# The first tokens' u half of a gated MLP by seven block products in place of eight, in a planned kernel

## The chip, the cores and the metric

The kernel runs on one core of a Trainium2 chip. The metric is device microseconds of one execution. Times are in microseconds (us) unless a text says otherwise.

## What is computed

Three layers in float32, for B = 2 batches, S = 768 tokens and a model width of 512 (8 heads of 64):

```python
for t in range(S):                       # retention, per head
    state = gamma * state + outer(k[t], v[t])
    y[t] = scale * (q[t] @ state)
# spectral mixing over tokens, then channels
theta = x @ w_theta
yr = einsum('ts,bsd->btd', w_tok_r, x * cos(theta))
yi = einsum('ts,bsd->btd', w_tok_i, x * sin(theta))
u = x + yr + yi
x = u + maximum(u @ w_ch, 0.0)
# gated MLP
h = gelu_tanh(x @ w_in)                  # 512 -> 1024
u, v = h[..., :512], h[..., 512:]
v_n = (v - mean(v)) / sqrt(var(v) + 1e-06) * g_ln
v_s = einsum('ts,bsd->btd', w_sg, v_n) + b_sg[None, :, None]
return x + (u * v_s) @ w_out
```

The change concerns `x @ w_in[:, :512]`, the u half.

## The kernel before, in words

**Precision.** Every operand of a large product is split into a high and a low half of a shorter float32 format: ScalarE rounds to the high half (`split_hi`, L331) and VectorE subtracts to get the low one (`split_lo`, L337). `terms3` then multiplies high by high, low by high and high by low: three matmuls for each 128-deep block, all recorded at L311. Weights come as 64-bit words and are unpacked on ScalarE (L403) and VectorE (L412, L423) before they are split.

**Tiling.** Activations lie with channels on the 128 partitions and tokens along the free axis. There are three token groups: the first 512 tokens of batch 0 (`xa[0]`), of batch 1 (`xa[1]`), and the last 256 of both (`xb`). A tile of a layer (`layer`) is 128 output channels by 512 tokens: 4 input blocks times 3 terms, 12 matmuls of 512 columns, into one of 8 PSUM banks.

**Stages.** For 12 chunks of 128 tokens: `retention` (scores, VectorE's masks at L503, the state's outer product, "attend" in a part by the state and a part by the masked scores) and `theta` (the angle product with two W_THETA blocks, sine and cosine on ScalarE, a transpose of x at L716). `mix_main` and `mix_rest` mix tokens. `channels` is the layer with w_ch, whose relu and add on VectorE (L845) make x2. `up_v` makes v tiles with tokens on partitions, `norm` and `norm_tile` normalize them, `up_u` makes the u tiles (a `layer`, then `gelu`: ScalarE square, VectorE L865, ScalarE tanh, VectorE L881). `gate_tile` mixes v over tokens and multiplies by u; `finish` and `finish_four` are the output layer.

**Seven products.** The output layer of the first tokens already has a block form in the kernel before. Input and output channels are cut in two halves each and the two batches take the place of the columns, so that a 2x2 by 2x2 block product needs seven products of blocks in place of eight. `sum_weights` makes four sums of weight blocks, `sum_tokens` four differences of token blocks, for each of two 128-channel pieces; each is split in halves as any operand is. `seven` runs the products (6 matmuls each) for j = 0, 1 in four banks, where the second product into a bank adds to the first; `both` saves the first pair's sum (a copy on ScalarE at L1139, an add on VectorE at L1144). `finish_four` adds up the results.

**Order.** Every step is an operation of `Plan` with an engine, a length and the buffers it uses. `ORDER` is a table of operation numbers; `Plan.schedule` walks it, gives each operation a start from the lengths and the buffers that come free, and the instructions are issued in the order of these starts. The engines then run their queues and wait by semaphores. Before 34 us of the plan (`WARM`), gaps in TensorE's queue are filled with matmuls on the identity whose results nobody reads (`keep_warm`). SP issues the loads and stores, POOL a state update and a few small steps.

Of the kernel before, what the change touches and what calls it, by code (L numbers as in the profile page):

```python
# [14 lines left out]
ALU = mybir.AluOpType  # L15
# [47 lines left out]
class Plan:  # L63
# [105 lines left out]


ORDER = [
# [48 lines left out]
]  # L220


# [1 line left out]
def retention_spectral_gmlp(  # L224
# [38 lines left out]
    def halves(dtype=F32):  # L263
        b = Buf("pair", dtype)
        return Half(b, 0), Half(b, 1)
# [35 lines left out]
    def x_tile(g, d):  # L301
        return xa[g][:, d, :] if g < B else xb[:, d].rearrange("p b t -> p (b t)")
# [546 lines left out]
        dve(512, relu, ps=True, r=[t], w=x_keys(g, e), prio=prio)  # L849
        split_x(x2hl, g, e, prio)  # L850

    def gelu(t, o, prio):

        s = Buf()
        act(
            512,
            lambda: A.activation(out=ap(s), in_=ap(t), func=AF.Square),  # L857
            ps=True,
            r=[t],
            w=[s],  # L860
            prio=prio,
        )
        dve(
            512,
            lambda: V.scalar_tensor_tensor(  # L865
                out=ap(s), in0=ap(s), scalar=1.0 / GA, in1=ap(t), op0=ALU.add, op1=ALU.mult
            ),
            ps=True,
            r=[t],
            w=[s],  # L870
            prio=prio,
        )
        act(
            512,
            lambda: A.activation(out=ap(s), in_=ap(s), func=AF.Tanh, scale=GA * GC),  # L875
            w=[s],
            prio=prio,
        )
        dve(
            512,  # L880
            lambda: V.scalar_tensor_tensor(  # L881
                out=ap(o), in0=ap(s), scalar=1.0, in1=ap(t), op0=ALU.add, op1=ALU.mult
            ),
            ps=True,
            r=[t, s],
            w=[o],
            prio=prio,
        )
# [91 lines left out]
    def up_u(g, f, prio):  # L980
        t = layer(W_INU, x2hl, g, f, prio)
        if f % 2 == 0:
            gu[g, f], gu[g, f + 1] = halves()
        gelu(t, gu[g, f], prio)
# [118 lines left out]
                split(res[i, n], lambda i=i, t=t: ap(t[i]), 512, prio, [t[i]])  # L1103
        return res

    def seven(base, src, hl, ws, ts, j, prio):

        z, w, x, y = (bank() for _ in range(4))

# [50 lines left out]
    def store(g, d, o, prio):  # L1160
# [10 lines left out]

        dma(256, put, r=[o], prio=prio)

    def finish_four(j, ws, ts, prio):
        z, x, y, u, v = seven(W_OUT, None, ghl, ws, ts, j, prio)

        def add(o, a, b, r, **k):
            dve(
# [88 lines left out]
    t = TE  # L1267
    for k in range(2):
        weight(W_INU + k, t - 10 + 5 * k)
        weight(W_INV + k, t - 7 + 5 * k)  # L1270
    for g in range(3):
        for e in range(NP):
            channels(g, e, t)
            t += 2.7
    for g in (0, 2, 1):
        for q in range(4):
            up_v(g, q, t)
            t += 2.7
        norm(g, t)
        for q in range(4):  # L1280
            norm_tile(g, q, t + 1)
        for f in range(NP):
            up_u(g, f, t)
            t += 2.7
    dma(384, lambda: nc.sync.dma_start(out=brow, in_=bvec), w=["brow"], prio=t - 20)
    dma(2, lambda: nc.sync.dma_start(out=gcol, in_=gvec), w=["gcol"], prio=t - 20)

# [6 lines left out]
        weight_sg(s, t - C['SGP'] + s)  # L1294
    for k in range(2):
        weight(W_OUT + k, t + 20 + 5 * k)
    for g in (2, 0, 1):
        for f in range(NP):
            gate_tile(g, f, t)
            t += 4.1  # L1300
# [116 lines left out]
```

## Time and profile before

| | |
|---|---|
| median of 3 runs | 370.33 us (369.91 to 370.38) |
| the profiled execution | 370.23 us, of which the span from first to last instruction is 368.5 |
| busy: TensorE / VectorE / ScalarE / POOL | 363.0 / 290.1 / 178.6 / 10.8 us |
| matmul records | 2,364 |
| granted TensorE clock, mean | 1.000 |
| DMA traffic | 39.08 MB; 306 to 413 GB/s in the first 55 us, under 230 after |

How to read it: a matmul's busy time includes its way through the array, so consecutive ones overlap; the step from one start to the next tells how fast they go. A float32 matmul that is not in the split format leaves two records. Most matmuls have one source line, L311, because a helper issues them, and are told apart by shape: 128x512 and 128x256 are the layers, 64x128 with 64 rows the scores, 64x64 the outer products.

### The profile page before, as it was taken

The page shows a single profiled execution, that of the slowest core. Times are in us where ns is not written, and L with a number is a line of the kernel's source. Part 1 is how long each engine was busy: PE and PEld are TensorE (multiplying, and loading weights), DVE is VectorE, ACT ScalarE, POOL GpSimd, SP SyncE. Part 2 cuts the span into 40 slices and gives each one's busy share as a digit, 9 for nine tenths or more (in the row PEclk, how much of TensorE's full clock was granted, in tenths as well). Part 3 has the DMA queues.
Part 4 walks back from the last instruction along what each step waited for, and adds up shares of the span by engine and source line. Part 5 has one row for each costly group of instructions (what it writes and reads, how often), then busy time and mean ns, then how long its engine had stood idle before and what let it go on. Part 6 is the DMA issues. An engine that isn't in the chain of part 4 may idle for free.

```text
span 368.5 us, 5764 instructions
## 1 busy us (share of the span) xinstructions
PE 363.0 (99%) x2364; PEld 311.7 (85%) x2364; DVE 290.1 (79%) x441; ACT 178.6 (48%) x298; POOL 10.8 (3%) x18
## 2 busy tenths in 40 slices
PE   8899999999999999999999999999999999999996
PEld 7788888788998988889988888888888889988885
DVE  3999999998886885775786434897999596899984
ACT  2767987742543566634343212437493744314300
POOL 1021010030001000000000000000000000000000
PEclk9999999999999999999999999999999999999999
DMA  7999990233433121414160000000000000000134
GB/s 306 410 413 407 410 384 6 88 141 121 166 114 116 34 84 34 166 30 161 68 223 6 2 0 0 2 1 0 0 2 0 0 2 1 3 0 2 58 114 171
DMA packets 10346, 39.08 MB, mean 106 GB/s; under 512 B 1360, under 2 KB 2384, under 8 KB 7888
## 3 DMA queue, kind: packets, MB, share of 16 engines
q1 hardware_dynamic: 10176, 38.67, 27.7%
q8 instruction: 18, 0.29, 0.3%
q10 hardware_dynamic: 144, 0.05, 0.1%
q14 instruction: 8, 0.07, 0.1%
HBM read 35.57 MB, written 3.15 MB: 105 GB/s over the span
## 4 chain that ended last, share of the span: by engine, by line
PE 95%; DMA 4%; DVE 0%; SPq 0%; issue 0%
PE banks L311 93%; DMA b<-qkv 3%; PE banks L716 1%; DMA dec<-decays 1%; DVE b L1231 0%; SPq L457 0%
## 5 line engine op out<-in xcount | busy, mean ns | idle before, releaser
L311 PE MATMUL banks<-b,b 128*128 128x512 f32 (+2 forms) x1776 | 327.3, 351 | 0.0
L311 PEld LDWEIGHTS banks<-b,b 128*128 128x128 f32 (+1 forms) x1776 | 276.4, 183 | 46.0 <-issue 1.2
L331 ACT ACTIVATE b<-b 128x512 fp32r<-128x512 f32 (+1 forms) x71 | 56.0, 815 | 67.4 <-DVE b L423 23.5
L337 DVE TENSOR_TENSOR b<-b,b 128x512 fp32r<-128x512 f32 (+1 forms) x71 | 62.4, 898 | 15.4 <-ACT b L331 9.2
L423 DVE SCALAR_TENSOR_TENSOR b<-b 128x1024 int32<-128x1024 int32 x32 | 38.8, 1224 | 0.8 <-ACT b L403 0.3
L331 ACT ACTIVATE b<-xa 128x512 fp32r<-128x512 f32 (+1 forms) x26 | 17.1, 670 | 25.4 <-DVE xa L845 15.9
L403 ACT ACTIVATE b<-b 128x1024 f32<-128x1024 f32 x16 | 18.6, 1160 | 11.6 <-DMA b<-wts 8.6
L857 ACT ACTIVATE b<-banks 128x512 f32<-128x512 f32 x24 | 13.7, 589 | 15.0 <-PE banks L311 15.0
L337 DVE TENSOR_TENSOR b<-xa,b 128x512 fp32r<-128x512 f32 (+1 forms) x26 | 19.1, 743 | 1.7 <-ACT b L331 1.6
L311 PE MATMUL banks<-b 64*128 64x128 f32 (+1 forms) x352 | 19.3, 256 | 0.8 <-DMA b<-qkv 0.8
L875 ACT ACTIVATE b<-b 128x512 f32<-128x512 f32 x24 | 14.7, 625 | 10.8 <-DVE b L865 10.8
L311 PEld LDWEIGHTS banks<-b 64*128 64x128 f32 (+1 forms) x352 | 17.1, 165 | 3.0 <-DMA b<-qkv 1.1
L865 DVE SCALAR_TENSOR_TENSOR b<-b,banks 128x512 f32<-128x512 f32 x24 | 15.9, 680 | 4.1 <-ACT b L857 4.1
L881 DVE SCALAR_TENSOR_TENSOR b<-b,banks 128x512 f32<-128x512 f32 x24 | 16.4, 682 | 2.6 <-ACT b L875 2.5
L724 DVE TENSOR_TENSOR b<-banks,b 128x1024 f32<-128x1024 f32 x12 | 14.7, 1223 | 3.9 <-ACT b L707 2.2
L526 ACT ACTIVATE b<-b,dec 128x64 f32<-128x64 f32 x56 | 14.1, 335 | 7.4 <-DMA b<-qkv 7.4
L503 DVE TENSOR_TENSOR b<-banks,causal 128x512 f32<-128x512 f32 x24 | 15.8, 686 | 1.7 <-PE banks L311 1.7
L412 DVE TENSOR_SCALAR b<-b 128x1024 int32<-128x1024 int32 x16 | 11.4, 717 | 4.2 <-DMA b<-wts 4.2
L331 ACT ACTIVATE b<-xb 128x512 fp32r<-128x512 f32 (+1 forms) x13 | 8.4, 663 | 12.3 <-DVE xb L845 8.7
L1036 DVE SCALAR_TENSOR_TENSOR b<-banks,gcol,brow 128x512 f32<-128x512 f32 x12 | 8.9, 749 | 5.5 <-PE banks L311 5.5
L845 DVE SCALAR_TENSOR_TENSOR xa<-banks,xa 128x512 f32<-128x512 f32 x8 | 5.5, 690 | 8.0 <-PE banks L311 7.9
L311 PE MATMUL banks<-b,state 64*64 64x128 f32 x160 | 10.9, 275 | 0.0
(66 smaller groups left out, 193.2 us busy)
## 6 DMA issues: line engine op xcount, KB each, us to landing
b<-wts SPq DMA_DIRECT2D x16, 1024.0 KB, 4.9
b<-qkv SPq DMA_DIRECT2D x24, 512.0 KB, 11.1
out<-b SPq DMA_DIRECT2D x11, 256.0 KB, 2.1
b<-wsg SPq DMA_DIRECT2D x9, 256.0 KB, 7.0
xa<-wts SPq DMA_DIRECT2D x2, 1024.0 KB, 11.2
xb<-wts SPq DMA_DIRECT2D x1, 1024.0 KB, 8.3
brow<-bvec SPq DMA_DIRECT2D x1, 384.0 KB, 11.4
dq<-qdecays SPq DMA_DIRECT2D x1, 256.0 KB, 6.4
```

The source lines that it names most:

```text
L311: nc.tensor.matmul(out=o, lhsT=l, rhs=r, start=start, stop=stop, skip_group_check=more)
L331: act(words, lambda: A.activation(out=hi(), in_=src(), func=AF.Copy), prio=prio, r=r, **k)
L337: lambda: E.tensor_tensor(out=lo(), in0=src(), in1=hi().bitcast(F32), op=ALU.subtract),
L403: lambda: A.activation(out=words(1).bitcast(F32), in_=words(1).bitcast(F32), func=AF.Copy, scale=REBIAS),
L423: lambda scalar=scalar, op=op: V.scalar_tensor_tensor(out=words(0), in0=words(1), scalar=scalar, in1=words(0), op0=op, op1=ALU.bitwise_or,),
L503: V.tensor_tensor(out=ap(at[i])[:, h * 512 + lo : h * 512 + hi].rearrange("p (n t) -> p n t", n=n), in0=ap(sc[h])[:, lo:hi].rearrange("p ( ...
L526: A.activation(out=v, in_=v, func=AF.Copy, scale=dk[:, h : h + 1])
L724: V.tensor_tensor(out=z2, in0=ap(tp)[:, None, :].to_broadcast([P, 2, 512]), in1=z2, op=ALU.mult)
L857: lambda: A.activation(out=ap(s), in_=ap(t), func=AF.Square),
L865: lambda: V.scalar_tensor_tensor(out=ap(s), in0=ap(s), scalar=1.0 / GA, in1=ap(t), op0=ALU.add, op1=ALU.mult),
L875: lambda: A.activation(out=ap(s), in_=ap(s), func=AF.Tanh, scale=GA * GC),
L881: lambda: V.scalar_tensor_tensor(out=ap(o), in0=ap(s), scalar=1.0, in1=ap(t), op0=ALU.add, op1=ALU.mult),
```

## The change

The u half of the first 512 tokens of both batches goes through `seven` as the output layer does. The operations: `sum_weights` and `sum_tokens` are called on W_INU and x2, and `up_four` adds the products up to the four results of each j and sends them through `gelu`; three of the four results now lie in SBUF, so `gelu` gets a switch that tells the planner so. `up_u` remains for the group `xb`. The weights of u are wanted earlier than those of v, u comes before v, and the gate takes the groups in the order 0, 2, 1. `ORDER` is a new table.

```diff
 ORDER = [
-    56, 58, 57, 85, 86, 59, 0, 114, 113, 60, 141, 142, 63, 62, 64, 61, 741, 87, 66, 7, 90, 88, 169,
...
+    56, 58, 57, 86, 85, 59, 113, 114, 0, 60, 169, 141, 63, 62, 64, 61, 197, 90, 65, 66, 142, 87, 7,
...
-    def gelu(t, o, prio):
+    def gelu(t, o, prio, ps=True):
...
-            ps=True,
+            ps=ps,
...
-    def seven(base, src, hl, ws, ts, j, prio):
+    def seven(base, hl, ws, ts, j, prio):
...
+    def up_four(j, ws, ts, prio):
+        z, x, y, u, v = seven(W_INU, x2hl, ws, ts, j, prio)
+        for g, f, part in ((0, j, z), (1, j, x), (0, 2 + j, y), (1, 2 + j, v)):
+            if f % 2 == 0:
+                gu[g, f], gu[g, f + 1] = halves()
+            t = part
+            if part is not z:
+                t = v if part is v else Buf()
+                dve(
+                    512,
+                    lambda t=t, part=part: V.tensor_tensor(
+                        out=ap(t), in0=ap(part), in1=ap(u), op=ALU.add
+                    ),
+                    ps=part is not v, r=[part, u], w=[t], prio=prio,
+                )
+            gelu(t, gu[g, f], prio, ps=part is z)
+
     def finish_four(j, ws, ts, prio):
-        z, x, y, u, v = seven(W_OUT, None, ghl, ws, ts, j, prio)
+        z, x, y, u, v = seven(W_OUT, ghl, ws, ts, j, prio)
...
         weight(W_INU + k, t - 10 + 5 * k)
-        weight(W_INV + k, t - 7 + 5 * k)
+        weight(W_INV + k, t + 30 + 5 * k)
     for g in range(3):
         for e in range(NP):
             channels(g, e, t)
             t += 2.7
+    ws = sum_weights(W_INU, t - 8)
+    ts = sum_tokens(lambda g, d: (lambda: x_tile(g, d), x_keys(g, d)), t - 4)
+    for f in range(NP):
+        up_u(2, f, t)
+        t += 2.7
+    for j in range(2):
+        up_four(j, ws, ts, t)
+        t += 9.5
     for g in (0, 2, 1):
         for q in range(4):
             up_v(g, q, t)
...
-        for f in range(NP):
-            up_u(g, f, t)
-            t += 2.7
...
-    for g in (2, 0, 1):
+    for g in (0, 2, 1):
         for f in range(NP):
             gate_tile(g, f, t)
```

Three places show how the instructions move. The first is SP's queue at the start, where `qkv` halves (512 KB) and W_THETA's first block (into `xb`) are loaded. Before:

```order
L457 DMA b_102<-qkv 128x1024
L482 DMA dq<-qdecays 128x512
L392 DMA xb<-wts 128x2048
L457 DMA b_106<-qkv 128x1024
L457 DMA b_108<-qkv 128x1024
```

Now:

```order
L461 DMA b_102<-qkv 128x1024
L486 DMA dq<-qdecays 128x512
L461 DMA b_105<-qkv 128x1024
L461 DMA b_107<-qkv 128x1024
L396 DMA xb<-wts 128x2048
```

The first W_THETA block stands two qkv halves further back.

The second is TensorE's queue up to the first angle product, a row of 128x512. 128x128 on a `b` buffer are scores, 64x64 an outer product, 64x128 an attend, `ident` alone a filler, `ident,xa` a transpose. Before:

```order
L311 MATMUL banks<-ident 128x128 x2
L716 MATMUL banks<-ident,xa_86 128x128 x4
L311 MATMUL banks<-b_102 64x64 x8
L311 MATMUL banks<-b_100,state_65 64x128 x8
L311 MATMUL banks<-b_166,b_102 64x128 x8
L311 MATMUL banks<-ident 128x128
L311 MATMUL banks<-b_108 128x128 x8
L311 MATMUL banks<-b_106 64x64 x8
L311 MATMUL banks<-b_121 128x128 x8
L311 MATMUL banks<-b_108,state_64 64x128 x8
L311 MATMUL banks<-b_247,b_106 64x128 x8
L311 MATMUL banks<-b_235,b_179 128x512 x2
```

Now:

```order
L315 MATMUL banks<-b_100 64x64 x8
L315 MATMUL banks<-b_105 128x128 x8
L315 MATMUL banks<-b_102,state_65 64x128 x8
L315 MATMUL banks<-b_183,b_100 64x128 x8
L315 MATMUL banks<-b_105,state_64 64x128 x8
L315 MATMUL banks<-b_223,b_107 64x128 x8
L315 MATMUL banks<-b_107 64x64 x8
L315 MATMUL banks<-b_121 128x128 x8
L720 MATMUL banks<-ident,xa_86 128x128 x8
L315 MATMUL banks<-b_123 128x128 x8
L315 MATMUL banks<-b_139 128x128 x8
L315 MATMUL banks<-b_278,b_173 128x512 x2
```

Two blocks of scores and one of transposes (four matmuls) more stand ahead of the angle product, and the third filler is gone.

The third is VectorE's queue in the channels' stage, up to the low halves for the first product on a token difference. L849 (L845 before) is the relu, L1099 a token difference, L341 a low half (L337 before); `xa_86` is batch 0, `xa_87` batch 1. Before, where the first relus of batch 0 stand:

```order
L845 SCALAR_TENSOR_TENSOR xa_86<-banks,xa_86 128x512
L337 TENSOR_TENSOR b_1906<-xa_86,b_1906 128x512
L337 TENSOR_TENSOR b_1831<-xb,b_1831 128x512
L845 SCALAR_TENSOR_TENSOR xa_86<-banks,xa_86 128x512
L845 SCALAR_TENSOR_TENSOR xb<-banks,xb 128x512
L337 TENSOR_TENSOR b_1911<-xa_86,b_1911 128x512
```

Now:

```order
L1099 TENSOR_TENSOR b_1930<-xa_87,xa_86 128x512
L849 SCALAR_TENSOR_TENSOR xa_86<-banks,xa_86 128x512
L1099 TENSOR_TENSOR b_1945<-xa_87,b_1930 128x512
L341 TENSOR_TENSOR b_1886<-xb,b_1886 128x512
L1099 TENSOR_TENSOR b_1948<-xa_87,xa_86 128x512
L341 TENSOR_TENSOR b_1892<-b_1572,b_1892 128x512
L341 TENSOR_TENSOR b_1963<-b_1948,b_1963 128x512
L341 TENSOR_TENSOR b_1965<-b_1930,b_1965 128x512
```

Seven rows run from the second batch-0 relu to the low half `b_1965`, which the first product on a token difference reads; 24 matmuls of two channel tiles stand on TensorE between that relu's tile and the product.

## Rows read from the trace of the kernel before

**Rows 1.** The page: span, and busy time of each engine.

```profile
span 368.5 us, 5764 instructions
...
PE 363.0 (99%) x2364; PEld 311.7 (85%) x2364; DVE 290.1 (79%) x441; ACT 178.6 (48%) x298; POOL 10.8 (3%) x18
```

**Rows 2.** The chain that ended last, in order of time: start, length (us), what.

```profile
5.12 11.40 DMA b<-qkv
...
49.24 0.44 PE banks L716 x4
...
130.49 234.79 PE banks L311 x1188
```

**Rows 3.** The waits of TensorE: total us, times, longest.

```profile
PE banks L311 <- DVE halfpi L273: 1.2, 1, 1.2
PE banks L311 <- DMA b<-qkv: 0.8, 2, 0.6
```

**Rows 4.** Timeline of TensorE, 200 to 222 us.

```profile
199.64 22.60 PE L311 MATMUL banks<-b,b 128*128 128x512 f32 x99
```

**Rows 5.** Timeline of TensorE, 3.5 to 20 us: start, us, instructions; idle before and releaser.

```profile
6.66 1.78 PE L311 MATMUL banks<-b 128*64 128x64 f32 x32
...
9.39 0.71 PE L311 MATMUL banks<-ident 128*128 128x128 f32 x4
...
10.84 0.69 PE L311 MATMUL banks<-b 128*64 128x64 f32 x16
11.46 1.09 PE L311 MATMUL banks<-b,state 64*64 64x128 f32 x16
12.48 1.09 PE L311 MATMUL banks<-b,b 128*64 128x128 f32 x16
...
16.56 1.16 PE L311 MATMUL banks<-b 64*128 64x128 f32 x16 [0.64 <-DMA b<-qkv]
17.65 1.09 PE L311 MATMUL banks<-b,state 64*64 64x128 f32 x16
18.67 1.52 PE L311 MATMUL banks<-b,b 128*64 128x128 f32 x17
```

**Rows 6.** The page and the DMA view: GB/s in 40 slices; a load of qkv.

```profile
GB/s 306 410 413 407 410 384 6 88 141 121 166 114 116 34 84 34 166 30 161 68 223 6 2 0 0 2 1 0 0 2 0 0 2 1 3 0 2 58 114 171
...
b<-qkv SPq DMA_DIRECT2D x24, 512.0 KB, 11.1
```

**Rows 7.** Timeline of TensorE, 37 to 49 us: three blocks of scores in a row.

```profile
38.40 2.95 PE L311 MATMUL banks<-b 64*128 64x128 f32 x48
41.28 1.09 PE L311 MATMUL banks<-b,state 64*64 64x128 f32 x16
```

**Rows 8.** Timeline of all engines, 9 to 20 us: the steps of a W_THETA block; two masks.

```profile
11.57 1.20 ACT L403 ACTIVATE xb<-xb 128x1024 f32<-128x1024 f32 x1 [0.56 <-DMA xb<-wts]
...
12.80 2.91 DVE L423 SCALAR_TENSOR_TENSOR xb<-xb 128x1024 int32<-128x1024 int32 x2
...
15.63 1.28 DVE L503 TENSOR_TENSOR b<-banks,causal 128x512 f32<-128x512 f32 x2
15.75 1.14 ACT L331 ACTIVATE b<-xb 128x1024 fp32r<-128x1024 f32 x1 [0.88 <-DVE xb L423]
...
17.42 1.22 DVE L337 TENSOR_TENSOR b<-xb,b 128x1024 fp32r<-128x1024 f32 x1
17.54 0.63 ACT L331 ACTIVATE b<-xa 128x512 fp32r<-128x512 f32 x1 [0.66 <-DVE xa L622]
```

**Rows 9.** Busy time by stretch: PE, PEld, DVE, ACT, POOL; granted clock; DMA.

```profile
134.00:154.00 20.00, 20.00 (x89) 16.54 (x89) 13.12 (x14) 12.30 (x18) 0.00 (x0) 1.00 0.26 93
...
194.00:214.00 20.00, 20.00 (x90) 16.57 (x89) 10.55 (x17) 6.22 (x10) 0.00 (x0) 1.00 0.00 1
214.00:234.00 20.00, 20.00 (x90) 16.57 (x89) 9.02 (x15) 4.93 (x10) 0.00 (x0) 1.00 0.00 0
```

**Rows 10.** The same view at the start.

```profile
10.00:20.00 10.00, 9.05 (x136) 7.45 (x136) 9.59 (x14) 7.83 (x23) 1.56 (x2) 1.00 1.02 405
```

More of the change, by code (lines that the diff above doesn't have):

```diff
@@ L867, in gelu @@
             ),
-            ps=True,
+            ps=ps,
             r=[t],
@@ L883, in gelu @@
             ),
-            ps=True,
+            ps=ps,
             r=[t, s],
```

98 rows, old and new, of the table ORDER are left out of this document.

## The prediction

> **What bounds the kernel now.** I read the busy times first, then the chain of waits, then TensorE's own waits and its timeline, and last VectorE's load by stretch. TensorE is busy 363.0 us of a 368.5 us span, VectorE 290.1, ScalarE 178.6 [rows 1]. A busy TensorE need not be a full one, so the chain matters more: after a load that lands at 16.5 us it is TensorE alone, with a last piece of 234.79 us and 1,188 matmuls that nothing interrupts [rows 2]. TensorE's two longest entries in the table of waits are 1.2 us for VectorE's first memset and 0.8 us for qkv loads, both before 17 us [rows 3]. And it is dense: 99 matmuls of 512 columns start within 22.60 us, 0.228 us each [rows 4]. So from 20 us on, a matmul taken away is time taken away, provided that VectorE and ScalarE, which make every operand, stay ahead. Before 20 us TensorE is short of data: it runs filler matmuls on the identity, at 9.39 for one, and waits before 16.56 [rows 5].
>
> **Twelve matmuls fewer.** The first tokens' u half had 8 tiles of 12 matmuls; now it has 14 products of 6, so 84 in place of 96. The order counts 1,128 matmuls of 512 columns before and 1,116 after, and every other kind of work as often as before. 12 x 0.228 = **2.7 us** off the path [rows 4]. The Trainium skill (TensorE: Matmul & The Clock Gate, Back-to-back issue gap) gives a sustained 131 ns per matmul of 512 columns; by it this term would be 1.6 us and the time 1.1 us longer. The trace does not agree: 0.228 is measured over 99 in a row, so the sum goes by that.
>
> **The head.** The loads are reordered: two more of the qkv halves (512 KB each) go ahead of the first W_THETA block. At 410 GB/s such a half takes 1.28 us [rows 6], so that block lands 2.6 us later, and the first angle product, which began at 18.67 + 1.02 = 19.7 us, can be late by that. TensorE has more to do meanwhile. The order puts two more blocks of scores and one more block of transposes ahead of the first angle product. Three blocks of scores in a row take 41.28 - 38.40 = 2.88 us and one alone 1.09 [rows 5, 7], so one more in a run is 0.90; a block of transposes is 0.44 [rows 2]. That moves 2 x 0.90 + 0.44 = **2.2 us** out of the dense part.
>
> When does the angle product start? Up to the first outer products nothing changes (7.3 us); two fillers, as at 9.39 before, take 0.9, which makes 8.2. Then stand three attends by the masked scores, two by the state, three single blocks of scores and a pair, two outers, two transposes. By the starts in [rows 5] half an attend is 1.02, scores 1.09, outer 0.62: 5 x 1.02 + 3 x 1.09 + (1.09 + 0.90) + 2 x 0.62 + 0.9 = 12.5 us, so 20.7. The last qkv half among them lands three halves behind the weight, at 14.1 + 3 x 1.28 = 18.0, before its scores are due at 19.7. Does the weight allow that? Before, the block landed at 11.57 and its low half was ready at 17.42 + 1.22 = 18.64, 7.1 us later; the five steps themselves (1.20, two in 2.91, 1.14, 1.22) are 6.5, the rest was waiting [rows 8]. From 14.1 that is 20.6 to 21.2, and the low half is wanted by the third matmul, 0.45 after the start: the weight allows 20.2 to 20.8. I take **20.7**, 1.0 later than before, since TensorE's own queue is about as long as the weight's; the late end is 19.7 + 2.6 = 22.3.
>
> **Shape changes.** TensorE loses a little whenever it goes from 64-row or 64-column tiles to full ones or to another kind: 1.09 - 0.90 = 0.19 us per run of scores [rows 5, 7]. Behind the first angle product I count 27 such places before and 25 after: 2 x 0.17 (an estimate, a little under the 0.19), **0.3 us**.
>
> **Sum.** From the first angle product to the last matmul: -2.7 - 2.2 - 0.3 = -5.2; it starts 1.0 later: **-4.2 us**. The tail keeps its form: the last tile still ends in two halves of 256 columns with one add and one store each. The profiled execution took 370.23 us, which gives 366.0; the median of the runs, 370.33, stands 0.1 above it: **366.1 us**.
>
> **What is costed at nothing.** VectorE gets 34 instructions of 512 words: 4 weight sums and 8 token sums, each with a low half, 4 adds of the shared pairs and 6 of the results. Two in a row take 1.28 us, so the second starts 0.60 after the first [rows 8]: 34 x 0.60 = 20 us. ScalarE gets 16 at 0.63 [rows 8], 10 us, of its 190 free. SP issues the same loads and stores, with W_INU's two blocks now ahead of W_INV's, and POOL scales gcol and brow behind the last state instead of between two; the first reader of those two, a gate tile, comes long after. The cover for VectorE is the stretch that held channels and the first up tiles: of 194 to 234 us it is busy 10.55 + 9.02 of 40 us, and 13.12 of 134 to 154, where the weight sums now stand [rows 9]. That is some 27 us free, and gelus for u now come earlier, into it. The thinnest place I find is the first product on a token difference: two tiles of channels (5.4 us) stand between the batch-0 tile it needs and it, and on VectorE seven instructions from that tile's relu to its own low half, 7 x 0.60 + 0.2 = 4.4; since the third matmul needs the low half, 1.3 us is left. Next in line are the copies of the first product of each pair: the accumulating product that reuses the bank waits for ScalarE, and behind it the whole of TensorE; by the same adding-up about 1.0 us is left there. From 10 to 20 us VectorE was busy 9.59 of 10 us [rows 10], and TensorE did not wait for it [rows 3]; the order puts no new instruction into that stretch or the next hundred microseconds, so it is no tighter there except by the 1.2 us (2.2 less 1.0) by which TensorE comes earlier.
>
> **Rivals.**
> *The loads set the head.* If the weight steps queue as badly as before, the angle product starts at 22.3: -5.2 + 2.6 = -2.6, **367.7 us**. For it: the weight's last step had 0.6 us of waiting in it before [rows 8], and it now shares VectorE with the masks of three blocks of scores. Against: each mask is 0.60, so the loads' case needs some three of them ahead of the low half. Chance 0.15.
> *Short waits in the new half.* The relay of tile, difference, high half, low half, product, copy, add loses its 1.0 to 1.3 us margins in two or three places: 1 to 3 us lost, near **368 us**. For it: margins of about 1 us on sums of 7 to 10 instructions. Against: the kernel before held its output half, with the same relay, without one wait [rows 3]. Chance 0.10.
> *Slower: VectorE arrives in arrears.* Place: the first product on a token difference. If the 24 instructions of the sums and their low halves (14.4 us) all stood in front of it, TensorE would wait 14.4 + 4.4 - 5.9 = 12.9 us: about **379 us**. It turns slower than before once VectorE is 5.5 us behind there (1.3 of margin and the 4.2 won), and 6.2 for a slowdown that shows. Against: from 134 to 154 us VectorE was busy 13.12 of 20 us [rows 9], so it has time to catch up. Chance 0.02.
> *The clock.* The granted clock was 1.00 from 10 to 20 us, with a wait of 0.64 us in them [rows 5, 10], so it is the 2.4 GHz level throughout; the new order has no longer wait, and one filler less. The Trainium skill (the same page, What's actually happening) says that full clock is released by activity and is not the resting state; no row here shows the lower level. If 5 us of the dense part ran at 1.2 GHz instead of 2.4, up to 5 us would be added: **371 us**. Chance 0.01.
> That the change does not take matmuls away is ruled out by the count in the order.
>
> **How the numbers follow.** The measurement tells about 0.2% (0.7 us) from no change. Forecast 0.72, then 0.15, 0.10, 0.02 and 0.01. Faster by over 0.2% means under 369.6: forecast, loads, and all but 0.02 of the short waits, 0.95. Within 0.2%: that rest and the clock, 0.03. Slower: 0.02. The range starts 0.7 below the forecast, 365.4: the 12.5 us of the head are a sum over 14 blocks, and 0.05 us on each is as much. It ends a little above the loads' case, at 368.0. That holds the forecast, the loads and part of the short waits.
>
> **What would show it.** Right: 2,350 matmul records on TensorE in place of 2,364 and a waits table without VectorE or ScalarE beyond the first 20 us; the first angle product near 20.7 us; the last matmul ending near 361 instead of 365.3; VectorE busy some 310 us, ScalarE 188, both idle less between 194 and 234 us. Wrong: a wait of TensorE for VectorE at the channels or the u products, a gap before the first angle product, or a granted clock under 1.00.

## The result, and the profile after

The changed kernel takes 367.06 us (median of 4 runs, 367.0 to 367.26) against 370.32 us; the ratio is 0.9915, with a 95% interval of 0.9898 to 0.9932. That is 3.3 us faster. The forecast was 366.1 in a range of 365.4 to 368.0, so the sign and the range held, and 1.0 us is missing. The measured time lies nearer to the loads rival (367.7) than to the forecast.

The page of the kernel after, beside [rows 1]:

```profile
span 365.3 us, 5796 instructions
...
PE 360.9 (99%) x2350; PEld 309.7 (85%) x2350; DVE 311.8 (85%) x475; ACT 187.0 (51%) x314; POOL 13.3 (4%) x18
```

The counts are as foretold: 2,350 matmul records, VectorE 311.8 us (about 310 forecast), ScalarE 187.0 (188). The waits of TensorE in the kernel after, beside [rows 3], are a single row: neither a load nor VectorE nor ScalarE is named behind the first memset.

```profile
PE banks L315 <- DVE halfpi L277: 1.2, 1, 1.2
```

The chain that ended last in the kernel after, beside [rows 2], is TensorE from 1.23 us on; its last piece:

```profile
150.49 211.66 PE banks L315 x1080
```

The work per stretch in the kernel after (columns as in [rows 9]) shows where VectorE took its new work in:

```profile
134.00:154.00 20.00, 20.00 (x92) 16.55 (x91) 16.48 (x18) 13.14 (x19) 0.00 (x0) 1.00 0.18 67
194.00:214.00 20.00, 20.00 (x90) 16.57 (x89) 17.03 (x28) 8.22 (x15) 0.00 (x0) 1.00 0.08 34
214.00:234.00 20.00, 20.00 (x90) 16.57 (x89) 17.26 (x28) 10.78 (x19) 0.00 (x0) 1.00 0.00 0
```

From 194 to 234 us VectorE goes from 19.6 to 34.3 us busy of 40 while TensorE stays at 20.00 of 20. So the cover that the prediction counted on was there, and most of it is now used.

Two points in time split the difference. The first angle product starts at 21.26 us (before 19.70; forecast 20.7), and the last matmul ends at 362.13 (before 365.26; forecast 361.06). What lies between shrank from 345.56 to 340.87 us, by 4.7 where 5.2 was forecast. So the missing 1.07 us is 0.56 at the start and 0.51 behind it. The timeline of TensorE in the kernel after, beside [rows 5]:

```profile
3.96 1.49 PE L315 MATMUL banks<-ident 128*128 128x128 f32 x6
5.37 1.16 PE L315 MATMUL banks<-b 64*128 64x128 f32 x16
...
8.36 1.09 PE L315 MATMUL banks<-b,b 128*64 128x128 f32 x16
...
17.83 1.10 PE L720 MATMUL banks<-ident,xa 128*128 128x128 f32 x8
18.86 2.47 PE L315 MATMUL banks<-b 64*128 64x128 f32 x32
21.26 2.12 PE L315 MATMUL banks<-b,b 128*128 128x512 f32 x7
```

The first attend starts at 8.36, where 8.2 was forecast. The last two blocks of scores, a pair at 18.86, last 2.40 us to the start of the angle product; a pair was priced at 1.99. And seven 512-column matmuls take 2.12 us from 21.26, as long as eight do in run 1 below: one matmul's time is lost. The timeline of the other engines in the kernel after, beside [rows 8], shows why:

```profile
15.46 1.21 ACT L407 ACTIVATE xb<-xb 128x1024 f32<-128x1024 f32 x1 [1.75 <-DMA xb<-wts]
16.70 2.49 DVE L427 SCALAR_TENSOR_TENSOR xb<-xb 128x1024 int32<-128x1024 int32 x2 [0.54 <-ACT xb L407]
...
19.10 0.68 DVE L626 TENSOR_TENSOR xa<-banks,dq 128x512 f32<-128x512 f32 x1
...
20.63 1.26 DVE L341 TENSOR_TENSOR b<-xb,b 128x1024 fp32r<-128x1024 f32 x1
...
21.95 0.99 PEld L315 LDWEIGHTS banks<-b,b 128*128 128x128 f32 x5 [0.39 <-DVE b L341]
```

The W_THETA block lands at 15.44 us, not at 14.1. Its five steps then run as priced (15.46 to 21.89, 6.4 us; 6.5 forecast), but 1.3 us later. Its two long steps on VectorE (L427) stand in front of L626 and a state update, which free the banks that the last scores write; so the pair of scores is held up, though only for some 0.2 us at a time, too short for the table of waits. And the third matmul of the angle product waits for the low half (L341), which shows on the weight loads alone (0.39 us). What made the block late is the question of the experiments; the first suspect is a transfer that no row of the program issues. The DMA view of the kernel after, 13.1 to 13.9 us:

```profile
DMA packets 76, 0.29 MB, mean 358 GB/s; under 512 B 15, under 2 KB 15, under 8 KB 69
...
q8 instruction: 1, 0.02, 8.7%
```

The last line is one packet of 16 KB of the instruction queue (the page has 18 of them, 0.29 MB), from 13.29 to 14.40 us; its 8.7% of 16 engines over 0.8 us are 1.1 us of one engine. The 15 under 512 B are 4-byte packets, here called marks: the trace has 16 of them, as many as there are DMA engines, before the landing of a load. The sixteenth mark ends at 14.41, right behind the fetch.

### The profile page after: what moved, and what is told of

The parts are those of the page before. It is cut to its first block, busy times and chain, and to the rows that moved or that the text cites. A ratio compares the mean times of both kernels' runs of the same rounds, so it can differ in the third digit from the quotient of the medians.

```text
span 365.3 us, 5796 instructions
## 1 busy us (share of the span) xinstructions
PE 360.9 (99%) x2350; PEld 309.7 (85%) x2350; DVE 311.8 (85%) x475; ACT 187.0 (51%) x314; POOL 13.3 (4%) x18
## 4 chain that ended last, share of the span: by engine, by line
PE 99%; DVE 0%; issue 0%
PE banks L315 97%; PE banks L720 1%; DVE b L1252 0%; DVE state L273 0%; DVE halfpi L277 0%
## 5 line engine op out<-in xcount | busy, mean ns | idle before, releaser
L315 PEld LDWEIGHTS banks<-b,b 128*128 128x128 f32 (+1 forms) x1764 | 273.6, 183 | 46.0 <-issue 1.5
L335 ACT ACTIVATE b<-b 128x512 fp32r<-128x512 f32 (+1 forms) x83 | 62.6, 787 | 58.0 <-DVE b L427 21.8
L341 DVE TENSOR_TENSOR b<-b,b 128x512 fp32r<-128x512 f32 (+1 forms) x83 | 70.6, 876 | 11.3 <-PE banks L315 7.0
L427 DVE SCALAR_TENSOR_TENSOR b<-b 128x1024 int32<-128x1024 int32 x32 | 38.8, 1220 | 0.4
L335 ACT ACTIVATE b<-xa 128x512 fp32r<-128x512 f32 (+1 forms) x26 | 17.1, 665 | 19.6 <-DVE xa L771 12.8
L341 DVE TENSOR_TENSOR b<-xa,b 128x512 fp32r<-128x512 f32 (+1 forms) x26 | 18.6, 725 | 4.0 <-ACT b L335 3.9
L315 PE MATMUL banks<-b 64*128 64x128 f32 (+1 forms) x352 | 19.6, 256 | 0.0
L530 ACT ACTIVATE b<-b,dec 128x64 f32<-128x64 f32 x56 | 14.1, 335 | 5.6 <-DMA b<-qkv 5.6
L970 ACT ACTIVATE b<-b,rstd 128x512 f32<-128x512 f32 x12 | 9.6, 808 | 8.6 <-DVE rstd L959 8.5
L885 DVE SCALAR_TENSOR_TENSOR b<-b,banks 128x512 f32<-128x512 f32 x18 | 12.2, 680 | 1.7 <-ACT b L879 1.3
L869 DVE SCALAR_TENSOR_TENSOR b<-b,banks 128x512 f32<-128x512 f32 x18 | 11.9, 678 | 1.1 <-ACT b L861 0.9
L574 POOL TENSOR_TENSOR state<-grown,dec 128x256 f32<-128x256 f32 x8 | 8.5, 1065 | 116.8 <-DVE grown L571 116.8
L676 ACT ACTIVATE b<-banks 128x512 int32<-128x512 f32 x12 | 7.1, 588 | 11.1 <-PE banks L315 11.1
L861 ACT ACTIVATE b<-banks 128x512 f32<-128x512 f32 x18 | 10.4, 593 | 4.5 <-PE banks L315 3.7
```

Source lines behind the costliest of these rows:

```text
L315: nc.tensor.matmul(out=o, lhsT=l, rhs=r, start=start, stop=stop, skip_group_check=more)
L335: act(words, lambda: A.activation(out=hi(), in_=src(), func=AF.Copy), prio=prio, r=r, **k)
L341: lambda: E.tensor_tensor(out=lo(), in0=src(), in1=hi().bitcast(F32), op=ALU.subtract),
L427: lambda scalar=scalar, op=op: V.scalar_tensor_tensor(out=words(0), in0=words(1), scalar=scalar, in1=words(0), op0=op, op1=ALU.bitwise_or,),
L530: A.activation(out=v, in_=v, func=AF.Copy, scale=dk[:, h : h + 1])
L869: lambda: V.scalar_tensor_tensor(out=ap(s), in0=ap(s), scalar=1.0 / GA, in1=ap(t), op0=ALU.add, op1=ALU.mult),
```

## The experiments

Ten kernels ran. The sixth is an edit of the kernel before, the eighth is the changed kernel itself, and the others are edits of the changed kernel.

**1. The twelve matmuls put back.**

```
                 terms = [(tile(n), tuple(ap(v, F32R) for v in b[n])) for n in range(2)]
+                if base == W_INU and o is z and first:
+                    terms3(ap(o), terms, True, True)
                 terms3(ap(o), terms, first, True, not first)
```

> The changed kernel with twelve matmuls of 512 columns put back: the first product of each j of the u half is computed twice. Order, loads and VectorE's work stay. Theory (a matmul in the dense part costs its 0.228 us): 367.06 + 2.7 = 369.8 us. Rival by the Trainium skill's 131 ns (TensorE: Matmul & The Clock Gate, Back-to-back issue gap): 368.6 us. Rival (something else sets the end there, the twelve are free): 367.1 us.

369.71 us (369.05 to 369.92, 11 runs), ratio to the kernel before 0.9981 (0.9972 to 0.9989). That is 2.65 us over the changed kernel: 0.22 us each. The 131 ns of the Trainium skill (TensorE: Matmul & The Clock Gate, Back-to-back issue gap) would have given 368.6, and does not hold here. The traces say the same without the medians: behind the first angle product the 512-column matmuls take, from start to start, 257.89 us here and 255.19 in run 2, 2.70 apart.

This run brought a second answer that was not asked for. Its program is the same up to the u half, but its block landed at 14.11. The fetch ran from 13.49 to 14.59, and by 13.60 all sixteen marks were there. The DMA view of this run, 13.1 to 13.9 us:

```profile
DMA packets 78, 0.29 MB, mean 358 GB/s; under 512 B 16, under 2 KB 16, under 8 KB 72
...
q8 instruction: 1, 0.02, 8.6%
```

The timeline of this run:

```profile
14.13 1.16 ACT L407 ACTIVATE xb<-xb 128x1024 f32<-128x1024 f32 x1 [0.47 <-DMA xb<-wts]
...
19.14 2.06 PE L315 MATMUL banks<-b 64*128 64x128 f32 x32
...
19.97 1.26 DVE L341 TENSOR_TENSOR b<-xb,b 128x1024 fp32r<-128x1024 f32 x1
...
21.12 2.11 PE L315 MATMUL banks<-b,b 128*128 128x512 f32 x8
```

The pair of scores takes 1.98 us, as priced, the low half is ready 0.1 us after the start, and the angle product starts 0.14 us earlier than in the changed kernel although TensorE's first attend came 0.29 later (8.65).

**2. Fillers half as many and twice as wide.**

```
-    for _ in range(6):
-        mm(warm[:, 0:P], states[0][:, 0:P], states[0][:, 0:P], True, True)
+    for _ in range(3):
+        mm(warm[:, 0 : 2 * P], states[0][:, 0:P], states[0], True, True)
...
-        for _ in range(n):
-            mm(banks[:, bank * 512 : bank * 512 + P], ident, ident, True, True)
+        for k in range(0, n, 2):
+            c = P * min(2, n - k)
+            mm(banks[:, bank * 512 : bank * 512 + c], ident, states[0][:, 0:c], True, True)
```

> The changed kernel with its early fillers half as many and twice as wide, so that TensorE's instruction stream is 12 matmuls and 12 weight loads shorter before 9 us and as long in time. Theory (the W_THETA block, whose packets end at 13.8 us but which lands at 15.44, is held up by the 16 KB instruction fetch of 13.29 to 14.40 us on one of the DMA engines, and it is this lateness that makes the scores and the low half late in front of the first angle product): the fetch comes some 0.7 us later, the block lands near 14.2, the first angle product starts near 20.9 in place of 21.26 without a second wait, the whole is 0.4 to 0.6 us shorter, 366.5 to 366.7 us. Rival (the loads are late for their bytes alone, or TensorE's own queue sets the start): the block lands at 15.4 again, 367.1 us.

The time did not move: 367.24 us (366.57 to 367.32, 4 runs). What was to be moved did move. The fetch came at 14.18, the block landed at 14.08, the pair of scores took 1.99 us, the angle product had no second wait, and everything behind it took 340.64 us in place of 340.87. But TensorE came to its speed late; the timeline of this run, beside the first two rows of the timeline after:

```profile
3.95 1.49 PE L315 MATMUL banks<-state,ident 128*128 128x256 f32 x4
5.37 2.08 PE L315 MATMUL banks<-b 64*128 64x128 f32 x16
```

The same 16 matmuls take 2.08 us in place of 1.16, and the rest is shifted by 0.9 (first attend 9.27). By the trace a gain of 0.65 us is there (0.42 at the start of the angle product and 0.23 behind it), and 0.9 of slow start takes it away. Whether the wide fillers made the start slow is not shown: it also differs between runs that share their fillers, as the last section shows.

**3. One token difference computed five times.**

```
+                def difference(o=t[i], x=x, y=y, k=extra(i, n)):
+                    for _ in range(1 + k):
+                        V.tensor_tensor(out=ap(o), in0=x(), in1=y(), op=ALU.subtract)
...
+        lambda g, d: (lambda: x_tile(g, d), x_keys(g, d)), t - 4, lambda i, n: 4 * (i == 0 and n == 1)
```

> The changed kernel with one of the token differences of the u half computed five times over: 4 instructions of VectorE, 0.60 us each, between the relu and the low half that the first product on a token difference waits for. In the changed kernel that low half ended 1.15 us before TensorE used it. Theory (VectorE's lateness is hidden to exactly that margin and then costs one for one): 4 x 0.60 - 1.15 = 1.25 us, 368.3 us, and one wait of TensorE for VectorE near 209 us. Rival (later joints have less margin and it is paid again there): 369.5 us or more. Rival (VectorE's free time behind it absorbs it): 367.1 us.

369.02 us (368.16 to 369.07, 5 runs; four lie within 0.06, and why the one at 368.16 is shorter is not known). The chain that ended last in this run, from the place on:

```profile
205.20 0.61 DVE b L1099
205.82 0.02 issue
205.84 0.70 DVE b L1099
...
208.80 0.64 ACT b L335
209.44 0.02 issue
209.46 1.30 DVE b L341 x2
210.77 0.04 issue
210.81 153.32 PE banks L315 x754
```

The place and the engine are right; two sizes were off. A repeat starts 0.73 us after the one before it, not 0.60: it writes the same tile, and in the trace it carries a wait for VectorE's own semaphore, so it starts when the other has ended. So VectorE is 2.9 us late, and 2.9 - 1.15 = 1.8 is what the margin leaves. TensorE lost 1.9 there (it waits first for the high half, then again for the low half, and each restart costs about 0.1). Nothing was paid again behind it: to the end, TensorE's starts lie 1.95 to 1.97 us later than in the changed kernel.

**4. Each of the eight token sums computed twice.** (The same edit with `lambda i, n: 1`.)

> The changed kernel with each of the eight token sums of the u half computed twice: 8 more instructions of VectorE, 4.8 us, two of them in front of the first product on a token difference. Theory (margin of 1.15 us there, and free time of VectorE behind it): 2 x 0.60 - 1.15 = 0.05 us, so 367.1 to 367.3 us and at most one short wait. Rival (VectorE is loaded to 17.7 us in 20 there, and 4.8 us more do not fit): TensorE waits, 368.5 us or more.

368.05 us (367.94 to 368.16, 5 runs): 1.0 more than the changed kernel, between theory and rival. At 0.73 each the two in front make 1.46, over the margin of 1.15 by 0.3. The table of waits shows none of it; TensorE's weight loads do:

```profile
208.72 0.30 PEld L315 LDWEIGHTS banks<-b,b 128*128 128x128 f32 x2 [0.27 <-ACT b L335]
209.52 19.82 PEld L315 LDWEIGHTS banks<-b,b 128*128 128x128 f32 x88 [0.51 <-DVE b L341]
229.85 1.23 PEld L315 LDWEIGHTS banks<-b,b 128*128 128x128 f32 x6 [0.50 <-ACT b L1139]
```

The matmuls near 209 us lose 0.46 us in all against the changed kernel, start by start, and those at 229.85 another 0.38; the second place is the bank whose copy on ScalarE (the second-thinnest place of the prediction) comes late. What follows: the new half runs without a wait, but with about 1 us of slack at both places.

**5. The old first part.** The first 270 entries of `ORDER` were put in the sequence that the same operations have in the kernel before; nothing else was changed.

> The changed kernel with the first 270 entries of its order (to about 80 us) in the sequence that the kernel before has: loads, scores, outer products, angle products stand as before, the u half by seven products and all behind it as changed. Theory from the two traces (the new first part starts its angle products 1.56 us later and has 2.7 us less work left then, but 0.7 us more in switches and short waits): it is worth about 0.4 us, so 367.5 us. Rival (the prediction's step: 2.2 + 0.3 - 1.0 = 1.5 us): 368.6 us. Rival (the first part is worth nothing, all is the seven products): 367.1 us.

367.49 us (367.04 to 367.9, 5 runs), 0.4 over the changed kernel, as the two traces had it; the runs spread by twice that. The first angle product starts at 19.49, and what follows takes 343.04 us: 1.77 earlier and 2.17 longer. In this execution no load that TensorE waited for was late, as told below. So of the 3.3 us won, some 0.4 is the new first part, where the prediction had 2.2 + 0.3 - 1.0 = 1.5; the rest came with the seven products and the layers reordered around them.

**6. The kernel before with twelve matmuls left out.**

```
-                    for d in range(NP)
+                    for d in range(NP - (base == W_INU and g == 0))
```

> The kernel before with twelve matmuls of 512 columns left out and nothing put in their place: the u half of the first batch's first 512 tokens leaves out the last of its four weight blocks, 3 matmuls in each of 4 tiles. Theory (0.228 us each, on the path in the kernel before too): 370.32 - 2.7 = 367.6 us; what the change gains beyond that, 0.5 us, is its order. Rival by 131 ns each: 368.7 us. Rival (they are hidden behind VectorE or ScalarE): 370.3 us.

368.29 us (368.03 to 368.72, 5 runs): 2.1 off, not 2.7. The timeline of TensorE in this run has a wait that the kernel before did not have:

```profile
239.75 8.09 PE L311 MATMUL banks<-b,b 128*128 128x512 f32 x35
248.35 1.88 PE L311 MATMUL banks<-b,b 128*128 128x512 f32 x7 [0.51 <-DVE b L337]
```

From start to start 0.78 us are lost at 247.5 us, where VectorE, behind its string of short normalisation steps, makes a low half: in the kernel before TensorE did not wait there, so in the old order the matmuls taken away were in part its cover. What came off up to the last matmul is 2.73 - 0.78 + 0.24 (the angle product started at 19.46) = 2.2 us, the profiled span's difference. So twelve matmuls are worth less in the old order than in the new one.

**7 and 8. Without the late fillers; and the changed kernel once more.**

```
-            if done < WARM and gap > (0.4 if done < 9.0 else 0.8):
+            if done < 5.0 and gap > 0.4:
```

> The changed kernel without its last two groups of fillers (at 6.46 and 7.72 us, 8 matmuls and 8 weight loads in all); TensorE waits in their place for the same operands. The early fillers, up to 5.3 us, stay as they are, so TensorE should come to full speed where it did. Theory (16 KB instruction fetch): the fetch comes after 16 instructions fewer, some 0.4 to 0.5 us later, near 13.75 us, when the packets of the W_THETA block are through; the block lands near 14.1 in place of 15.44, the first angle product starts near 20.85 in place of 21.26 and does not wait a second time; 0.4 to 0.6 us shorter than the changed kernel on the same chip. Rival (landing time follows from the bytes): no difference. Rival (the pauses cost TensorE its speed, as the wide fillers seem to have): the first matmuls behind them take up to twice as long, slower than the changed kernel.

> The changed kernel itself once more, beside the run before it. All theories: 367.0 to 367.3 us. What it is for: whether the moment at which TensorE comes to full speed (between 4.1 and 7.3 us in the runs so far), the fetch and the landing of the W_THETA block move together from one execution to the next: fetch at 13.3 with a landing at 15.4, fetch at 13.5 with 14.1, as in two of the runs so far.

367.01 us (366.82 to 367.2) without them, 367.09 (366.9 to 367.21) for the kernel itself: no difference, and neither theory nor second rival. The fetch came at 13.43 (in the repeat at 13.22), 0.1 to 0.2 later and not 0.4 to 0.5, and the block landed at 15.57 (15.36). My reckoning that the fetch comes so many instructions later fell with this run. TensorE lost no speed by the pauses.

**9 and 10. One and two fillers more.** (`keep_warm` of the group at 7.7 us with 1 and 2 more.)

> The changed kernel with one filler more (two matmuls, 0.22 us) in front of the first attend, which delays everything TensorE does up to the first angle product. Seen so far: the instruction fetch comes at the start of one and the same attend (13.2 to 13.5 us), whatever fillers stand before; the W_THETA block lands 2.14 us behind the fetch where it came by 13.43 (five executions), and at 14.1 where it came at 13.49 or later on the same chip (two). Theory: the fetch comes near 13.5 to 13.6, just late enough; the block lands at 14.1, the angle product starts 12.48 us behind the attend, at 21.07, without a second wait (0.25 us): 0.4 us shorter than the changed kernel in such executions, 0.2 longer in those where it is hit all the same. Rival (the fillers only take time): 0.2 us longer, 367.3 us.

> The same with two fillers more (0.44 us). Theory: the fetch comes at 13.65 or later and misses the block for certain: it lands at 14.1, the angle product starts at 8.81 + 12.48 = 21.29, as late as in the changed kernel, but nothing waits behind it: 0.2 us shorter, 366.8 us. Rival (the fillers only take time): 0.4 us longer, 367.5 us.

367.12 us (366.74 to 367.52) and 367.27 (366.68 to 367.5): neither tells itself from the changed kernel. In the profiled executions the fetch came at 13.25 and 13.33, not at 13.5 or later, and hit the block (15.40 and 15.62). So these runs did not make the miss that they were meant to make, and no version that beats the changed kernel was found.

The nine executions that share the new order's first part can be laid side by side. Times are us, from the traces; "behind" is from the first angle product to the last matmul, less the 2.73 of the first run and without the two in which VectorE was slowed later on:

| run | fetch | block lands | first attend | angle product | less landing | less attend | behind |
|---|---|---|---|---|---|---|---|
| changed kernel | 13.29 | 15.44 | 8.36 | 21.26 | 5.82 | 12.90 | 340.87 |
| same again | 13.22 | 15.36 | 8.37 | 21.19 | 5.83 | 12.83 | 340.89 |
| four late | 13.30 | 15.45 | 8.27 | 21.28 | 5.83 | 13.01 | |
| eight late | 13.52 | 15.66 | 8.47 | 21.48 | 5.82 | 13.01 | |
| no late fillers | 13.43 | 15.57 | 8.43 | 21.39 | 5.82 | 12.95 | 340.89 |
| one filler more | 13.25 | 15.40 | 8.59 | 21.22 | 5.82 | 12.64 | 340.87 |
| two fillers more | 13.33 | 15.62 | 8.54 | 21.44 | 5.82 | 12.90 | 340.90 |
| twelve back | 13.49 | 14.11 | 8.65 | 21.12 | 7.01 | 12.48 | 340.60 |
| wide fillers | 14.18 | 14.08 | 9.27 | 21.75 | 7.67 | 12.48 | 340.64 |

In the first seven the angle product starts 5.81 to 5.83 us behind the landing, whatever TensorE did before; in the last two 12.48 us behind the first attend, whenever the block landed. The later of the two sets the start, and a block that is hit costs another 0.25 us behind it. In each of the seven, 15 marks had ended by 13.8 us and the sixteenth followed the fetch; in the two, all 16 had ended by 13.6. The moment of the fetch alone does not decide: at 13.52 in run 4 it hit the block, at 13.49 in run 1 it did not, and in run 4 the marks stand about 0.1 us later.

## Why the prediction was right, and what it mis-sized

**Right: twelve matmuls, 2.7 us.** Put back they cost 2.65. This gain rests on TensorE being dense and the rest staying ahead, and it did: no row for VectorE or ScalarE in the waits behind the first memset.

**Right: what was costed at nothing.** The two thin places were where they were said to be. The low half of the first product on a token difference ended 207.81 and was used at 208.95, 1.15 us of margin (1.3 forecast, though its own terms, 5.4 + 0.45 - 4.4, make 1.45); at the copies of the first products it was 1.04 (1.0 forecast). Runs 3 and 4 show these margins from the other side. The rivals of arrears, clock and short waits did not occur in the new half; the trace's record of full clock runs from 5.35 us past the last matmul.

**Right in kind: two blocks of scores and one of transposes moved ahead.** Added up by starts, the part behind the first angle product has 2.02 us of scores and 0.48 of transposes less, 2.5 (2.2 forecast).

**Mis-sized: the step "lands 2.6 us later", from which 14.1.** It came 3.9 us later, at 15.44, in seven of nine executions. The sum of bytes was right: in the two executions that the fetch spared the block landed at 14.1. And the reckoning of TensorE's queue, 12.5 us from attend to angle product, was right too: 12.48 there. What the step left out is the instruction fetch, 1.1 us on one DMA engine while the block's last packets were due. The same lateness stood in the trace before: the fetch of 14.02 fell on a qkv half, which landed at 16.52 in place of about 15.3 and is the load that TensorE waited 0.64 us for [rows 5]. Runs 5 and 6, which have the old first part, show it: there the fetch came at 14.71 and 14.92, the same half landed at 15.33, and TensorE ran its three blocks of scores without a wait. Its timeline in run 6:

```profile
14.61 2.87 PE L311 MATMUL banks<-b 64*128 64x128 f32 x48
```

I had read the row of the kernel before and put the delay down to the load, not to a moment in time that the new order would fill with another load. It costs 21.26 - (8.36 + 12.48) = 0.42 at the start and 0.25 behind it, 0.67 us of the 1.07. The loads rival (367.7) went in this direction, for another reason: the steps did not queue, their start was late. The qkv halves behind the block were late with it: the last one that the head needs landed at 19.14 (18.0 forecast), 0.04 us before the scores on it began, and cost nothing only by that little.

**Mis-sized: 8.2 for the first attend.** It was 8.36, 0.16 later. Up to the first outer products things did change: the fillers at 3.96 took 1.49 us, before 0.92, since TensorE came to its speed later in this execution, and the outer products ended at 7.72 in place of 7.3; the two fillers behind them then took 0.64, not 0.9. The moment of full speed differs from run to run, as below.

**Mis-sized: shape changes, 0.3 us.** They cost 0.3 us instead. In run 2, which the fetch spared, the part behind the first angle product is 345.56 - 340.64 = 4.92 us shorter than in the kernel before. Scores and transposes make 2.5 of it and one run of outer products fewer 0.2; the 512-column matmuls shrank by 2.23 us, not by 2.73. I counted the changes to and from half tiles, 27 and 25; but the order also splits the runs of 512-column matmuls more often (20 runs, before 15), and five more runs cost 0.5 us, 0.1 each. So -5.2 became -4.92: the 0.3 more from the moved blocks hides a part of this miss. The three terms, 0.67 + 0.16 + 0.28, are 1.1 us, and the forecast missed 1.07.

That the fetch holds up the load it meets is shown by all twelve traces, the kernel before and runs 5 and 6 included: in each, of the loads that land between 8 and 21 us exactly one lands 1.1 to 1.5 us behind the pace of the others, and it is the first load whose sixteenth mark came only behind the fetch. In runs 1 and 2 that was the qkv half behind the block (16.59 and 16.50). No run took the fetch away, and a kernel that is faster for missing it was not made. What stays open is what sets its moment. In all nine executions it came within 0.2 us of the start of the second attend by masked scores (13.21 in the changed kernel), so it goes with TensorE's progress; the 18 fetches for 4,700 TensorE records, matmuls and weight loads together, suggest that they bring TensorE's own program. But taking 16 or 24 of these records away ahead of it (runs 7 and 2) did not move it to a later matmul.

## What to carry to other kernels

A work item taken from a dense engine is worth its start-to-start time only if the engines that feed it have slack where they now must be earlier: twelve matmuls were worth 2.7 us in the new order and 2.0 in the old one, where VectorE was the next to be late. A load's landing is not its bytes alone; where a trace shows one load late for no reason of its own, ask at what moment that happened, and which load the new order will have there. Short waits of 0.1 to 0.3 us stood in no table of waits here: a 512-column matmul counts as busy for 0.39 us and the next one starts 0.23 after it, so a start that is a little late leaves little or no idle time. Look at the weight loads, or add up the starts.

## What was not expected of the hardware

- An instruction fetch of 16 KB took 1.1 us of one of 16 DMA engines, and the block in flight then landed 2.14 us behind the start of the fetch (2.29 in run 10): 1.3 us later than its bytes would have had it. The later loads of the changed kernel stayed late by 1.1 us or more; a second fetch at 20.5 us moved no landing. The landing came 1.03 us behind the block's sixteenth mark, in run 1 only 0.51; why is not shown.
- TensorE starts slowly, and the moment it comes to speed varies from one execution to the next. Twelve records of 128 columns took 2.93 us at 1.23 us, four 0.71 at 6.46. With the same fillers the first scores took 1.16 us when they started at 5.37 in the changed kernel, 1.45 in run 1, and 2.08 with the wide fillers of run 2; the view by stretch prints a granted clock of 1.00 (2.4 GHz) for all of them. But the packed trace holds no record of the clock ahead of a first one, and that view counts time without a record as 1.00. The first record, of full clock, begins at 5.35 us in the changed kernel, 6.00 in run 1 and 7.45 in run 2: ahead of these scores, in the middle of them, and behind them. In the kernel before it begins at 4.12. The Trainium skill (TensorE: Matmul & The Clock Gate, What's actually happening) says that full clock is not the resting state; the durations and these records agree.
- Instructions of VectorE on 512 words start 0.60 us apart although each takes 0.68, but 0.73 apart where each waits for VectorE's own semaphore because it writes the same tile (5 in 3.59 us).
